# A T5-bias attention kernel gets a new beginning: bias rows copied inside SBUF, last tokens scored first, loads in another order

## The chip, the cores and the metric

One core of a Trainium2 chip runs the whole program. The metric is device time in microseconds (us), the median of several executions. A core has five engines with queues of their own, each worked off strictly in order: PE (matrix products), ACT (exponentials, copies), DVE and POOL (elementwise work), SP (here only the starting of DMAs). [...] DMAs can be started from SP, ACT and POOL.

## The reference

Attention with a relative-position bias, then a mixture of low-rank adapters on its output. The sizes are B = 8 batches, H = 8 heads, S = 576 tokens, D = 64.

```python
scores = q @ k.T / sqrt(D) + bias_table[bucket(|i - j|)]   # per batch and head
attn = softmax(scores)
x = (attn @ v) as (B*S, H*D)                               # (4608, 512)
logits = x @ w_gate                                        # 8 experts, the best 2 chosen
out = x + sum over the 2 of softmax weight * (x @ A[e]) @ B[e]
```

From a distance of 128 tokens on all buckets are the last one, so a bias relative to the last bucket is zero there.

## The kernel before, in words

**Units.** A unit is a batch and a pair of heads; there are 32 (`NU`), four (`HP`) to a batch, taken in order. The 576 tokens are split into 512 main tokens and 64 last ones ("tail"). For each unit q and k are loaded (`load`, fp32 staging with four buffers each), cast to bf16 (`cast`, mostly on POOL), and turned by PE (`turn`, whose PSUM result DVE copies out). The tails of a whole batch are loaded at once (`load_tail`, two buffers), cast by `cast_tail`, and turned as an item of the same `turn`.

**Scores.** `edges(u)` scores the main tokens against the last ones and the other way round, one PSUM tile and one exponential of 128x1024 (`pt`). `keys(u, c)`, for c in 0, 2, 1, 3, scores 128 keys against 512 queries for two heads; the bias near the diagonal is added by four more matmuls from the table `Wt` (a Toeplitz-like row, shifted by one from partition to partition) against `anti`, and ACT exponentiates it into `pk`. `edges`, `keys` and `turn` share three PSUM tiles in rotation (`score_tile`); V products and small items share two others (pool `mp`). The bias of the edges is not added but multiplied after the exponential: `edge_l` (POOL) by the factors `EL`, `edge_t` (DVE) by `ET`, and the corner (last tokens against last tokens) by `EC` in `corners_bias` (POOL).

**The bias tables.** The 8x32 bias table is loaded, turned into rows `gx` (8x520) and `gp` (8x7x128, seven shifted and strided copies) by DVE and POOL. `gp` is written to DRAM (`gd`), and `table(h)` reads unit 0's part of `Wt` back for each head, 64 partitions each a shifted piece; `table_rest` reads the parts of the other three head pairs. `gx` is written to DRAM too (`gnd`), `table_n` reads `Wn`, and `factors_l`, `factors_t` and the second half of `corners_first` multiply it by `anti` and let ACT exponentiate EL, ET and EC.

**V products.** `step(u, j)` (j = 0, 1) multiplies the probabilities by V with a column of ones (`values`), and `normalise` divides. Around these steps the loop puts the matmuls of the adapters.

**Order.** It is written out by hand; there is no scheduler. Every engine's queue has the order of the source lines. The loop over u runs from 0 to 29; in round u the order is: casts for unit u+2 and v of unit u+1 on POOL (`prep`), tail loads and `load(u+4)` on SP, `edges(u)`, two `keys(u)`, `step(u-1, 0)`, `edge_l`, `edge_t`, two more `keys(u)`, `turn` of unit u+2, `step(u-1, 1)`. `prep` also casts the tails of batch 2 at u = 3 (table `tq`), and the adapter weights are cast by POOL in the same round (`weights_cast`). The last two units have their own code. A DMA from SP or ACT is released only when the DMA eight places before it in program order has landed.

The lines that matter below: L112 (q loads), L109 (k and v loads), L129 and L123 (tail loads), L141 and L137 (casts), L149 and L153 (tail casts), L201 (`table`), L205 (`table_rest`), L210 (`table_n`), L371 and L373 (turn: PE, DVE copy), L423 and L428 (keys: products, bias), L431 (exponential of keys), L500 and L502 (edges: PE, exponential), L507 (`edge_l`), L644 (`gp` to DRAM), L275 (weights cast).

Of the kernel before, what the change touches and what calls it, by code (L numbers as in the profile page):

```python
# [38 lines left out]
def kernel(  # L39
# [76 lines left out]
    def load_tail(b, names="qkv", g0=0, g1=HP):  # L116
        eng = nc.sync
# [45 lines left out]
    load_tail(0, "qk", 0, 1)  # L163
# [9 lines left out]
    nc.vector.memset(gp, 0.0)  # L173
    bts = cp.tile([H, NB], FP32, tag="bts")
# [3 lines left out]
    lo, runs = half, []  # L178
    for d in range(half + 1, FAR + 1):
        if d == FAR or buckets[d] != buckets[lo]:  # L180
            runs.append((lo, d))
            lo = d
    for i, (lo, d) in enumerate(runs):
        eng = (nc.vector, nc.gpsimd)[i % 2]
        eng.tensor_copy(gx[:, C + lo:C + d],
                        bts[:, buckets[lo]:buckets[lo] + 1].to_broadcast((H, d - lo)))
    nc.vector.tensor_copy(gx[:, C - FAR + 1:C], _ap(gx, C + FAR - 1, [[-1, FAR - 1]]))
    x0, xn = (C - FAR) // 4 - 1, FAR // 2 + 2
    nc.vector.tensor_copy(gp[:, :, x0:x0 + xn], _ap(gx, 4 * x0 + 1, [[1, 7], [4, xn]]))
    gd = nc.dram_tensor("g_d", (H, 7, GY), BF16, kind="Internal").ap()  # L190
# [9 lines left out]
    def table(h, eng):  # L200
        eng.dma_start(out=Wt[h * 64:h * 64 + 64, 0, :WN],  # L201
                      in_=_dram(gd, h * 7 * GY, [[1, 32], [2 * GY, 2], [1, WN]]))
# [4 lines left out]

# [8 lines left out]
    def factors_l():  # L216
        ps = score_tile("fl")
        for hp in range(HP):
            for e in range(2):
                for h in range(2):  # L220
                    rows = slice(h * 64, h * 64 + 64)
                    for f in range(2):
                        nc.tensor.matmul(ps[f * 64:f * 64 + 64, h, hp * 64 + e * 32:hp * 64 + e * 32 + 32],
# [3 lines left out]
        nc.scalar.activation(EL.rearrange("p g h x -> p h g x"),  # L227
                             ps[:, :, :HP * 64].rearrange("p h (g x) -> p h g x", g=HP), ACT.Exp,
                             scale=scale)

    def factors_t():
        ps = score_tile("ft")
        pst = ps.rearrange("p h (g x) -> p h g x", x=64)
        for hp in range(HP):
            for e in range(2):
                for h in range(2):
                    rows = slice(h * 64, h * 64 + 64)
                    nc.tensor.matmul(pst[64:, h, 2 * hp + e, :], lhsT=turned(h),
                                     rhs=Wn[rows, hp, 129 - e:193 - e],
                                     start=(hp == 0 and e == 0), stop=True,  # L240
                                     skip_group_check=True)
        nc.scalar.activation(ET[64:].rearrange("p g h x -> p h g x"),  # L242
                             ps[64:].rearrange("p h (g x) -> p h g x", g=HP), ACT.Exp, scale=scale)

    def presets():
        nc.vector.memset(ET[:64], 1.0)
        for t in pts:
            nc.gpsimd.memset(t[:, :64], 0.0)
        for i in range(2):
            nc.gpsimd.memset(tvs[i], 0.0)  # L250
            nc.gpsimd.memset(pcs[i], 0.0)
# [15 lines left out]
    def weights_load():  # L267
        nc.sync.dma_start(out=A4f.rearrange("p e c r -> p e (c r)"),
                          in_=moe_A.rearrange("e (p c) r -> p e (c r)", c=4))
        nc.sync.dma_start(out=G4f.rearrange("p c e -> p (c e)"),  # L270
                          in_=moe_w_gate.rearrange("(p c) e -> p (c e)", c=4))
        nc.sync.dma_start(out=Bf, in_=moe_B.rearrange("e r d -> (e r) d"))
# [195 lines left out]
    def corners_first(b):  # L468
        sc = score_tile("cn")
        n = HP * 64  # L470
        corner_scores(b, sc[:, 0, :n], 0, HP, True)
        for hp in range(HP):
            for e in range(2):
                for h in range(2):
                    rows = slice(h * 64, h * 64 + 64)
                    nc.tensor.matmul(_ap(sc[rows, 0, :], n + hp * 64 + e, [[2, 32]]),
                                     lhsT=Wn[rows, hp, 1 - e:65 - e], rhs=turned(h)[:, :32],
                                     start=False, stop=True, skip_group_check=True)
        px = ep.tile([128, HP, 64], BF16, name="pcx", tag="pcx")
        nc.scalar.activation(px.rearrange("p g i -> p (g i)"), sc[:, 0, :n], ACT.Exp, scale=scale)  # L480
        nc.scalar.activation(EC, sc[:, 0, n:2 * n], ACT.Exp, scale=scale)
        return px
# [159 lines left out]

    cast(0, "q", nc.scalar)
    nc.scalar.dma_start(out=gd, in_=gp)  # L644
    load(1, "qk")
    load(0, "v")
    cast_tail(0, "qk", nc.gpsimd, 0, 1)
    cast(0, "k", nc.gpsimd)
    turn([qk_item(0), tl_item(0, 0, 1)])
    for h in range(2):  # L650
        table(h, nc.scalar)
    nc.sync.dma_start(out=gnd, in_=gx)
    load_tail(0, "qk", 1)
    load_tail(0, "v")
    for h in range(2):
        table_n(h, nc.sync)
    cast_tail(0, "qk", nc.gpsimd, 1)
    presets()
    cast(1, "q", nc.vector)
    cast(1, "k", nc.vector)  # L660
# [11 lines left out]
    cast(0, "v", nc.gpsimd)  # L672
    cast_tail(0, "v", nc.gpsimd)

    tturn = {max(4 * c - 4, 2): c for c in range(1, B)}
    tload = {max(w - 2, 0): c for w, c in tturn.items()}
# [6 lines left out]
    def prep(u):  # L683
        b, hp = units[u]
        if u + 2 < NU:
            for nm in ("q", "k") if u > 0 else ("k",):
# [36 lines left out]
    for u in range(NU - 2):  # L723
        b, hp = units[u]
        open_probs(u)
        if u:
            prep(u)
        if u in tload:
            load_tail(tload[u])
        if u == 1:  # L730
            weights_load()
        if u + 4 < NU:
            load(u + 4)
        if u == 3:
            weights_cast()
# [3 lines left out]
        if u in (4, 5):  # L739
            weights_turn(u - 4)  # L740
# [235 lines left out]
```

## Time and profile before

| | |
|---|---|
| median of 3 runs | 200.79 us (199.09 to 200.93) |
| the profiled execution: time, span | 200.43 us, 198.6 us |
| busy: PE, DVE, ACT, POOL | 168.4, 131.1, 163.0, 124.0 us |
| DMA | 40.82 MB, 206 GB/s over the span |
| mean granted TensorE clock | 0.961 |

The span runs from the first to the last instruction on the core. A row of the timeline has the start, the time, the engine (a q behind it means its queue, where DMAs are issued), the line, the operation, output and input, and in brackets how long the engine had been idle and what ended that.

### The profile page before, as it was taken

What the parts mean: (1) busy time and instruction counts of PE and PEld (TensorE: products, weight loads), DVE (VectorE), ACT (ScalarE), POOL (GpSimd) and SP (SyncE); (2) the same over time, 40 slices, a digit from 0 to 9 for tenths busy, and PEclk for the clock granted to TensorE, in tenths of its full rate; (3) what the DMA queues carried; (4) which work ended last, traced back from release to release, by engine and by line L of the source; (5) the groups of instructions that cost most, each with busy time, mean ns of one, the idle gap of its engine ahead of it and who ended that gap; (6) DMA issues with size and microseconds to landing.
All of it is one profiled execution on the core that took longest, in us unless ns stands there. A gap on an engine that the chain in (4) does not pass through costs nothing. (4 is left out here: it accounts for less than half of the span.)

```text
span 198.6 us, 9888 instructions
## 1 busy us (share of the span) xinstructions
PE 168.4 (85%) x4230; PEld 128.1 (65%) x4253; DVE 131.1 (66%) x327; ACT 163.0 (82%) x204; POOL 124.0 (62%) x303
## 2 busy tenths in 40 slices
PE   0364999999999999999999999999999999996660
PEld 0233666777777777776777777776777777875430
DVE  4411244476577778788877787778786887896541
ACT  3148589999999999999999999999999999982331
POOL 4298543876586859594949494959585847243510
PEclk9999589999999999999999999999999999999965
DMA  5878989888888688857888888778898511132425
GB/s 136 219 217 261 233 214 251 259 251 239 242 240 244 163 250 275 264 154 235 222 262 245 244 265 251 219 184 250 254 296 264 161 56 53 56 104 75 149 95 169
DMA packets 68515, 40.82 MB, mean 206 GB/s; under 512 B 22248, under 2 KB 63736, under 8 KB 68472
## 3 DMA queue, kind: packets, MB, share of 16 engines
q1 hardware_dynamic: 67752, 39.77, 69.2%
q8 instruction: 33, 0.54, 1.1%
q10 hardware_dynamic: 720, 0.43, 0.8%
q14 instruction: 10, 0.08, 0.1%
HBM read 30.72 MB, written 9.46 MB: 202 GB/s over the span
## 5 line engine op out<-in xcount | busy, mean ns | idle before, releaser
L431 ACT ACTIVATE pk<-sc 128x1024 bf16<-128x1024 f32 x120 | 113.5, 1035 | 4.2 <-PE sc L428 4.2
L423 PE MATMUL sc<-tx 64*64 64x512 bf16 x480 | 49.5, 400 | 0.0
L373 DVE COPY tx<-tx 128x2048 bf16<-128x2048 bf16 (+8 forms) x36 | 36.3, 1007 | 15.0 <-PE tx L371 13.3
L526 PE MATMUL pv<-v,pk 128*128 128x65 bf16 x992 | 41.7, 194 | 4.1 <-PE sc L428 1.9
L428 PE MATMUL sc<-Wt,anti 64*64 64x256 bf16 x480 | 41.9, 307 | 3.2 <-DMA Wt<-g_d 3.2
L502 ACT ACTIVATE pt<-sc 128x1024 bf16<-128x1024 f32 x32 | 32.8, 1024 | 12.5 <-PE sc L500 6.7
L526 PEld LDWEIGHTS <-pk 128*128 128x128 bf16 x1024 | 37.7, 98 | 7.4 <-issue 1.8
L566 DVE TENSOR_TENSOR xn<-pv,rc 128x320 bf16<-128x320 f32 x62 | 30.5, 491 | 2.1
L565 DVE RECIPROCAL rc<-pv 128x5 f32<-128x5 f32 x62 | 11.9, 192 | 20.3 <-PE pv L573 11.0
L589 POOL TENSOR_TENSOR a<-z,top 128x16 f32<-128x16 f32 (+2 forms) x16 | 3.5, 222 | 34.4 <-DVE top L579 30.8
L304 DVE TENSOR_TENSOR ot<-dl,xn 128x512 f32<-128x512 f32 x26 | 17.9, 689 | 10.4 <-PE sc L428 9.4
L423 PEld LDWEIGHTS <-tx 64*64 64x64 bf16 x480 | 16.3, 108 | 10.2 <-issue 1.1
L428 PEld LDWEIGHTS <-anti 64*64 64x64 bf16 x480 | 18.5, 110 | 4.0 <-issue 3.9
L141 POOL CAST qn<-qs 128x512 bf16<-128x512 f32 x29 | 17.8, 612 | 4.8 <-DMA qs<-in_q_dram 4.8
L371 PEld LDWEIGHTS <-qn 64*128 64x128 bf16 x256 | 7.8, 97 | 20.0 <-issue 7.7
L137 POOL CAST v<-vs 128x512 bf16<-128x512 f32 x32 | 19.9, 623 | 0.9 <-PE pv L545 0.8
L141 POOL CAST kn<-ks 128x512 bf16<-128x512 f32 x31 | 19.0, 613 | 0.3 <-DMA ks<-in_k_dram 0.2
L371 PE MATMUL tx<-ident,qn 64*128 64x64 bf16 x256 | 9.7, 196 | 10.5 <-ACT qn L141 4.9
L543 PE MATMUL pv<-v,pt 128*128 128x65 bf16 x248 | 17.8, 195 | 0.0
L534 PE MATMUL pv<-vb,pt 128*128 128x130 bf16 x124 | 17.6, 225 | 0.0
L512 DVE TENSOR_TENSOR pt<-pt,ET 128x256 bf16<-128x256 bf16 x32 | 13.3, 415 | 4.1 <-ACT ET L242 4.1
L507 POOL TENSOR_TENSOR pt<-pt,EL 128x128 bf16<-128x128 bf16 x32 | 13.8, 432 | 0.7 <-ACT pt L502 0.2
(133 smaller groups left out, 286.5 us busy)
## 6 DMA issues: line engine op xcount, KB each, us to landing
qs<-in_q_dram SPq DMA_DIRECT2D x32, 256.0 KB, 3.7
vs<-in_v_dram SPq DMA_DIRECT2D x64, 128.0 KB, 4.1
out_dram<-ot SPq DMA_DIRECT2D x32, 256.0 KB, 2.6
ks<-in_k_dram SPq DMA_DIRECT2D x62, 128.0 KB, 4.0
vt<-in_v_dram SPq DMA_DIRECT2D x16, 128.0 KB, 3.5
out_dram<-ot SPq DMA_DIRECT2D x8, 128.0 KB, 3.1
qkt<-in_q_dram SPq DMA_DIRECT2D x7, 128.0 KB, 3.9
qkt<-in_k_dram SPq DMA_DIRECT2D x7, 128.0 KB, 4.0
```

Source lines behind the costliest of these rows:

```text
L137: eng.tensor_copy(t[:, :, :, :D].rearrange("p c h d -> p h c d"), s)
L141: copy(t.rearrange("p c h d -> p h c d"), s)
L304: nc.vector.tensor_tensor(ot.rearrange("p (g x) -> p g x", g=HP), dl.rearrange("p (g x) -> p g x", g=HP), x[:, j, :, 2 * f:2 * f + 2, :].r ...
L373: nc.vector.tensor_copy(sb[:, :n], ps.rearrange("p a (c i) -> p c a i", i=64)[:, :n])
L423: nc.tensor.matmul(sc[prt, h, :], lhsT=kT[rows, c * 128 + f * 64:c * 128 + f * 64 + 64], rhs=qT[rows, :], start=True, stop=False, skip_gro ...
L428: nc.tensor.matmul(_ap(sc[prt, h, :], p0, [[128, 4], [1, n]]), lhsT=turned(h), rhs=_ap(Wt[rows, hp, :], (1 - e) * GY + y0, [[GY, 4], [1, n]]),
L431: nc.scalar.activation(probs[u][0][:, c, :, :], sc, ACT.Exp, scale=scale)
L502: nc.scalar.activation(probs[u][1][:, 64:], sc.rearrange("p h x -> p (h x)"), ACT.Exp, scale=scale)
L526: nc.tensor.matmul(pv[:, o:o + W1], lhsT=pk_slice(u, c, h, j + 2 * f), rhs=vm[:, c, h, :], start=first, stop=False, skip_group_check=True)
L534: nc.tensor.matmul(_ap(pv, h * W1, [[130, 2], [1, W1]]), lhsT=probs[u][1][:, x0:x0 + 128], rhs=tvs[b % 2][:, 2 * hp + h].rearrange("p f d ...
L543: nc.tensor.matmul(pv[:, o:o + W1], lhsT=probs[u][1][:, x0:x0 + 128], rhs=vts[u % NV][:, c, h, :], start=False, stop=False, skip_group_che ...
L566: nc.vector.tensor_tensor(xs[b][:, j, hp], _ap(pv, 0, [[W1, 5], [1, D]]), _ap(rc, 6 * j, [[1, 5], [0, D]]), op=ALU.mult)
```

## The change

The loop starts at u = 3; what rounds 0 to 2 did is written out ahead of it in a new order. In it:

- `table(h)` copies straight from `gp` in SBUF, two DMAs per head, one for every second partition, from SP (h = 1) and ACT (h = 0). `gp` still goes to DRAM, from SP, for `table_rest`.
- The row `gx` is exponentiated once (`ge`, 8x520) and written to DRAM; `Wn` then holds exponentials, and DVE copies EL, EC and ET from PSUM instead of ACT exponentiating them.
- `edges(0)` and `edges(1)` come ahead of unit 0's keys; `edges(2)` ahead of unit 1's. The first V products come after unit 1's keys.
- Nine matmuls on zeros run on PE at the very start.
- Loads: the tails of batch 0 whole at once; k of unit 1 from ACT; q of unit 2 ahead of the tables; v tails of batch 0 and the adapter weights from POOL; v loads later; tails of batch 2 (q, k, v) after q and k of unit 6 and v of unit 5.
- DVE makes all runs of `gx`, and clears the `vb` tiles (128x1040 each) ahead of that; POOL clears `pc`.
- In the loop only the places of `weights_cast` (after `edge_l` of u = 3) and `weights_turn` (end of u = 4, and u = 5) differ.

```diff
     def table(h, eng):
-        eng.dma_start(out=Wt[h * 64:h * 64 + 64, 0, :WN],
-                      in_=_dram(gd, h * 7 * GY, [[1, 32], [2 * GY, 2], [1, WN]]))
+        for i in range(2):
+            eng.dma_start(out=Wt[h * 64 + i:h * 64 + 64:2, 0, :WN],
+                          in_=_ap(gp[h:h + 1], 2 * GY * i, [[1, 32], [1, WN]]))
...
+    def cast_half(u, nm, h, eng):
+        if h == 0:
+            nat[(u, nm)] = qkp.tile([128, 4, 2, D], BF16, name=f"{nm}n", tag=f"{nm}n")
+        copy = eng.copy if eng is nc.scalar else eng.tensor_copy
+        copy(nat[(u, nm)][:, :, h, :], stage[(u, nm)][:, h].rearrange("p (c d) -> p c d", c=4))
+
+    busy = mp.tile([128, 512], FP32, name="busy", tag="mm")
+    for _ in range(9):
+        nc.tensor.matmul(busy, lhsT=zero[:, :128], rhs=zero, start=True, stop=True, skip_group_check=True)
...
     cast(0, "q", nc.scalar)
-    nc.scalar.dma_start(out=gd, in_=gp)
-    load(1, "qk")
+    cast_tail(0, "qk", nc.gpsimd, 0, 1)
+    load(2, "q")
+    table(1, nc.sync)
+    table(0, nc.scalar)
+    nc.sync.dma_start(out=gd, in_=gp)
+    nc.scalar.activation(ge, gx, ACT.Exp, scale=scale)
+    nc.scalar.dma_start(out=gnd, in_=ge)
+    load(2, "k")
     load(0, "v")
...
     turn([qk_item(0), tl_item(0, 0, 1)])
...
+    cast(1, "q", nc.vector)
+    open_probs(0)
+    open_probs(1)
+    edges(0)
+    turn([qk_item(1), tl_item(0, 1, HP)])
+    edges(1)
     for h in range(2):
         table_n(h, nc.sync)
...
     for h in range(2):
         for i in range(2):
             table_rest(h, i, nc.sync)
-    load(2, "qk")
+    load(3, "qk")
     load(1, "v")
-    load(3, "qk")
+    load_tail(1, "qk")
+    load(4, "qk")
     load(2, "v")
+    presets()
+    load_tail(0, "v", eng=nc.gpsimd)
+    weights_load(nc.gpsimd)
+    nc.vector.memset(ET[:64], 1.0)
+    cast(2, "q", nc.vector)
+    cast(2, "k", nc.vector)
+    cast(0, "v", nc.gpsimd)
+    load_tail(1, "v")
+    load(5, "qk")
     load(3, "v")
+    for c in KO:
+        keys(0, c)
+    turn([qk_item(2)])
+    open_probs(2)
+    factors_l()
+    edges(2)
+    edge_l(0)
+    keys(1, KO[0])
+    factors_t()
+    edge_t(0)
+    keys(1, KO[1])
+    load(4, "v")
+    load(6, "qk")
+    px = corners_first(0)
+    cast_tail(0, "v", nc.gpsimd)
+    corners_bias(0, px)
...
+    for c in KO[2:]:
+        keys(1, c)
+    cast(3, "q", nc.gpsimd)
+    cast(3, "k", nc.gpsimd)
+    step(0, 0)
+    keys(2, KO[0])
+    cast(1, "v", nc.gpsimd)
+    load(5, "v")
+    load_tail(2)
+    step(0, 1)
+    keys(2, KO[1])
+    turn([qk_item(3)])
...
+    load(6, "v")
+    keys(2, KO[2])
+    step(1, 0)
+    keys(2, KO[3])
+    turn([qk_item(4), tl_item(1)])
+    step(1, 1)
...
-    for u in range(NU - 2):
+    for u in range(3, NU - 2):
```

The order of POOL's work in rounds 3 and 4 is now: q, k of unit 5, v of unit 4, tail casts (qk of batch 2, v of batch 1), `edge_l(3)`, the three weight casts, q, k of unit 6.

More of the change, by code (lines that the diff above doesn't have):

```diff
@@ L468, in corners_first @@
     def corners_first(b):
[L469 to L478, printed above, removed]
+        ps = mp.tile([128, 512], FP32, name="cn", tag="mm")[:, :HP * 64]
+        corner_scores(b, ps, 0, HP, True)
         px = ep.tile([128, HP, 64], BF16, name="pcx", tag="pcx")
-        nc.scalar.activation(px.rearrange("p g i -> p (g i)"), sc[:, 0, :n], ACT.Exp, scale=scale)
-        nc.scalar.activation(EC, sc[:, 0, n:2 * n], ACT.Exp, scale=scale)
+        nc.scalar.activation(px.rearrange("p g i -> p (g i)"), ps, ACT.Exp, scale=scale)
         return px
```

135 lines of the change are left out of this document (62 added, 73 removed).

## The prediction

> **What bounds the kernel now.** I read the 40 slices first, then the windows, then each engine in order of time.
>
> ```profile
> ACT  3148589999999999999999999999999999982331
> DMA  5878989888888688857888888778898511132425
> ```
>
> ACT, which exponentiates, is full from slice 6 to slice 34. Five exponentials make a unit (one `edges`, four `keys`), and 32 units run one after the other. So the question is when ACT first gets fed without holes, and whether it stays fed.
>
> ```profile
> L431 ACT ACTIVATE pk<-sc 128x1024 bf16<-128x1024 f32 x120 | 113.5, 1035 | 4.2 <-PE sc L428 4.2
> ```
>
> That is 113.5/120 = 0.946 us for each exponential in a row; one unit is 4.7 us and a little more.
>
> ```profile
> 5.19 0.60 ACTq L644 DMA_DIRECT2D g_d<-gp  x1
> 7.64 1.44 ACTq L201 DMA_DIRECT2D Wt<-g_d  x2
> ...
> 12.73 1.94 ACT L431 ACTIVATE pk<-sc 128x1024 bf16<-128x1024 f32 x2 [2.57 <-PE sc L428]
> ...
> 17.05 0.41 ACT L481 ACTIVATE EC<-cn 128x256 bf16<-128x256 f32 x1
> 17.31 0.63 ACT L227 ACTIVATE EL<-fl 128x512 bf16<-128x512 f32 x1
> 17.96 1.02 ACT L242 ACTIVATE ET<-ft 64x1024 bf16<-64x1024 f32 x1
> 21.39 1.02 ACT L502 ACTIVATE pt<-sc 128x1024 bf16<-128x1024 f32 x1 [2.41 <-PE sc L500]
> ...
> 32.42 1.02 ACT L502 ACTIVATE pt<-sc 128x1024 bf16<-128x1024 f32 x1 [0.18 <-issue]
> ...
> 42.59 1.02 ACT L502 ACTIVATE pt<-sc 128x1024 bf16<-128x1024 f32 x1 [0.24 <-DVE rc L565]
> ```
>
> The holes of the beginning are here: ACT waits for the bias table (until 12.73), spends 2.06 us on the factors EC, EL, ET, and waits for unit 1's projections (until 21.39). The edges of units 3 and 5 start at 32.42 and 42.59, 5.1 us a unit. The changed kernel enters its loop at unit 3 in the state that the old one has there (units 0 to 2 exponentiated, units 0 and 1 multiplied by V, q and k of unit 4 turned), and runs nearly the same loop. So the change is worth what those starts move.
>
> But DMA is nearly full too, and at 35 us it sets POOL's pace:
>
> ```profile
> 0.00:5.00 5.00, 0.12 (x6) 0.12 (x8) 2.13 (x14) 1.90 (x2) 2.15 (x15) 1.00 0.53 137
> 5.00:10.00 5.00, 1.91 (x34) 1.01 (x33) 2.44 (x5) 0.86 (x1) 1.30 (x4) 1.00 0.80 218
> 10.00:15.00 5.00, 3.21 (x46) 1.78 (x49) 0.89 (x1) 2.14 (x4) 4.76 (x18) 1.00 0.78 221
> 15.00:20.00 5.00, 1.91 (x80) 1.53 (x72) 0.98 (x2) 3.96 (x6) 4.10 (x9) 0.91 0.88 259
> 20.00:25.00 5.00, 4.84 (x79) 3.50 (x83) 1.50 (x5) 2.86 (x3) 2.81 (x5) 0.50 0.92 234
> 25.00:30.00 5.00, 5.00 (x116) 3.19 (x108) 2.40 (x7) 4.38 (x5) 2.21 (x4) 0.91 0.84 213
> 30.00:35.00 5.00, 4.62 (x118) 3.37 (x115) 2.46 (x7) 4.82 (x6) 1.79 (x3) 1.00 0.89 243
> 35.00:40.00 5.00, 4.56 (x114) 3.76 (x117) 2.19 (x7) 4.93 (x7) 4.56 (x9) 1.00 0.90 268
> ```
>
> (The last two columns are the share of the 16 DMA engines and GB/s.)
>
> ```profile
> 35.31 0.61 POOL L149 CAST qkb<-qkt 128x512 bf16<-128x512 f32 x1 [1.73 <-DMA qkt<-in_k_dram]
> 35.87 1.29 POOL L153 CAST vb<-vt 64x512 bf16<-64x512 f32 x2
> ...
> 38.65 0.42 POOL L507 TENSOR_TENSOR pt<-pt,EL 128x128 bf16<-128x128 bf16 x1
> ...
> 39.57 0.61 POOL L141 CAST kn<-ks 128x512 bf16<-128x512 f32 x1
> ```
>
> POOL waits for the last tokens of batch 2 until 35.31, then works through its queue until k of unit 6 is cast at 40.18. PE turns that k at once:
>
> ```profile
> 40.46 0.28 PE L371 MATMUL tx<-ident,kn 64*128 64x64 bf16 x8
> ```
>
> So at unit 4 the old kernel already stands 0.28 us from a DMA limit: landing of that load, plus 4.87 us on POOL, is the turn of unit 6.
>
> **The change part by part.**
>
> *The beginning.* The table for unit 0 no longer goes through DRAM: the wait from 5.19 (g_d issued) to 7.64 (it can be read back) goes. Against that, DVE now clears two 128x1040 tiles ahead of the bias rows and makes all 15 runs itself.
>
> ```profile
> 1.15 0.43 DVE L173 MEMSET gp<- 8x448 uint32 x1
> 3.16 0.23 DVE L175 TENSOR_SCALAR bts<-btT 8x32 f32<-8x32 f32 x1 [1.58 <-DMA btT<-in_bias_table_dram]
> 3.50 0.66 DVE L185 CAST gx<-bts 8x3 bf16<-8x3 f32 x8
> 4.73 0.43 DVE L189 COPY gp<-gx 8x462 bf16<-8x462 bf16 x1
> 7.49 0.91 DVE L246 MEMSET ET<- 64x1024 bf16 x1 [0.15 <-issue]
> ```
>
> After the clears of `zero` (0.28, as `gx` by its width), gx and gp, near 1.86, two clears at 0.93 (from 0.91 for 1024 columns) end near 3.7, 0.5 later than bts could start; 7 more runs at 0.66/8 cost 0.6, of which 0.35 was a wait for POOL anyway. gp is ready near 5.9 instead of 5.16. The four copies leave on ACT and SP from 5.9 to 7.2 and, at the 3.1 to 3.7 us that table loads take, land by 9.0 to 10.9.
>
> ```profile
> Wt<-g_d SPq DMA_DIRECT2D x4, 114.0 KB, 3.1
> ...
> Wt<-g_d ACTq DMA_DIRECT2D x2, 76.0 KB, 3.7
> ```
>
> Unit 0's edges start near 8.9 (the last-token loads are four times larger, but ACT issues its two copies earlier), unit 1's near 11.4, unit 0's keys near 12.3. From 11.4, 14 exponentials and one corner take 14 x 0.946 + 0.4 = 13.6 us, to 25.0. I add 1.6 for the rest of the table (issued to 14.3, so it lands at 17.4, when ACT would have wanted it near 16) and 1.2 for the four V products of units 0 and 1 that PE now has to fit between unit 2's keys. Unit 3's edges: about 27.8 instead of 32.42, bounds 26 and 31.5: the later one if PE keeps the 0.50 clock that the 20 to 25 us row shows, the earlier one without the holes. The factors leave ACT (one 8x520 row instead, at 7.3 where ACT is idle); DVE's six copies of them lie under keys of unit 1. That is 4.6 us gained, up to here. The nine warm-up matmuls run before 5.1, where PE has nothing else.
>
> *The loads.* The built program lets a DMA of SP or ACT go only when the one eight places before it has landed, as before. In the new order the last tokens of batch 2 come after q, k of unit 6 and v of unit 5, not before unit 6; the MoE weights and the last v tokens of batch 0 go through POOL's own queue. Bytes that SP's stream needs ahead of the cast at 35.31: 512 KB more (q, k of unit 6). POOL's order in unit 3 is unchanged up to there: q5, k5, v4, then this cast; after it vb, EL, the three weights, q6, k6 — the same 4.87 us. So units 4 and later can gain only as much as this load lands earlier.
>
> ```profile
> 28.08 0.38 SPq L112 DMA_DIRECT2D qs<-in_q_dram  x1
> ...
> 30.56 0.60 SPq L129 DMA_DIRECT2D qkt<-in_q_dram  x1
> 31.21 0.64 SPq L129 DMA_DIRECT2D qkt<-in_k_dram  x1
> ...
> 33.93 0.57 SPq L112 DMA_DIRECT2D qs<-in_q_dram  x1
> ...
> 36.61 0.47 SPq L112 DMA_DIRECT2D qs<-in_q_dram  x1
> ```
>
> By issue: the five DMAs of a unit take 2.48 (28.08 to 30.56) to 2.68 us (33.93 to 36.61), at most 0.54 each, one of last tokens 0.65 (30.56 to 31.21). SP after: gp at 5.9, two table copies 1.3, g_d 0.6, k2 and v0 2.0, Wn 1.3, rest of the table 2.55, waits for landings 0.65: 14.3. Ahead of the load in question stand 22 DMAs of units at 0.54 and five of last tokens at 0.65, 15.1 us; with 0.6 for waits by the eight-places rule (my choice) it is issued near 30.0 and lands 4.1 later (31.21 to 35.31): 34.1. By bytes: full-rate time used to 35.0 was the sum of share x 5, 28.2 us; 512 KB more at 268/0.90 GB/s is 1.7, so 29.9. With POOL's queue filling 10 to 17 us (shares 0.78 there now), 0.94 from 5 us on gives 34.0, and 0.89, what 30 to 35 had, gives 35.6. I take 34.3. Gain: 35.31 - 34.3 + 0.28 = 1.3 us. What the beginning gains beyond that is given back as a wait of PE for POOL at unit 4; the beginning may be some 2 us later than worked out and cost nothing. (EL of unit 3 stands behind this cast on POOL, 0.56 + 1.29 + 0.42 us, ready at 36.6; unit 4's first V product, which needs it, would be due some 1.5 us after unit 4's edges at 27.8 + 5.1, at 34.4.)
>
> *POOL's DMAs.* No row shows one. SP's take 0.4 to 0.65 us, POOL's longest instruction now is the 1.29 above: five cost 2 to 6.5 us from 9 us on. POOL's next work, v of unit 0, lands near 14, so up to 5 us are hidden; the rest falls in the 2 us of slack. I charge nothing, and 0 to 1 in the range.
>
> *The copies out of two partitions.* All 156 KB come from partitions 0 and 1. Lower bound of their price: as the DRAM loads above. Upper: if one sixteenth of the machine serves them, 268/0.90/16 = 18.6 GB/s, 8.4 us, landed at 15 instead of 10, and the four loads on SP behind them (each waits for one of them) 5 us late. I take the lower, since their issue and size are nearest to those rows, and keep the upper as a rival. [...]
>
> *Sum.* Profiled span 198.6; the profiled execution took 200.43, so 1.83 lies around it.
>
> ```profile
> core 0: 198.6 us, clock 0.961
> ```
>
> 198.6 - 1.3 + 1.83 = 199.1 us. The median of the three runs, 200.79, is 0.36 above that execution. Under 1%, about 2 us, this kernel's measurement tells no difference.
>
> **Rivals.** (a) *The load stream runs earlier.* If SP is through the tables by 13 and DMA keeps a share of 0.98 (for: the 5 to 15 us windows have room, and POOL's queue fills it; against: 0.92 is the best window of the first 40 us), the load lands at 32.8 and the gain is 2.8: 197.6. It can't be the whole 4.6, for that needs a landing at 31.0, a microsecond after its issue.
> (b) *Nothing reaches the end.* With a share of 0.89 the load lands at 35.6, 0.3 later than now, which the 0.28 covers, and unit 4 waits for POOL exactly where it does now: 200.4, though unit 3 starts 4 us sooner.
> (c) *Slower: the copies inside SBUF.* If the four land after 11.6 instead of 10, SP, which waits for each of them before v0 and Wn, runs late by the difference, and at 1.3 us of it the gain is gone. At the upper price, 5 us less 1 that POOL's queue moves meanwhile, the stream is 4 late: 199.1 + 4 = 203.1. For: two partitions are all of the source. Against: each copy is only 39 KB.
>
> **How the numbers follow.** Forecast 0.38 (198.3 to 200.0), (a) 0.30, (b) 0.12, (c) 0.20. Faster by over 1% means below 198.4: all of (a) and a fifth of the forecast, 0.38. Slower by over 1%: (c) but for its mild part, 0.17. The rest, 0.45. The range for 8 in 10 takes in most of (a), down to 196.3, and most of (c), up to 202.6.
>
> **What would show it.** Right: unit 3's edges at 26 to 31.5, PE's turn of unit 6 waiting for POOL, POOL's cast of batch 2's last tokens waiting for DMA until 33.5 to 35, and from unit 5 on a constant lead of 1 to 2 us. The copies: unit 0's first bias matmul at 9.5 to 11 (right) or after 12 (rival c). Wrong: a lead above 3 us at unit 6, or unit 3 not ahead, or units longer than 5.3 us in the middle of the run.

## The result, and the profile after

The changed kernel takes 210.04 us (median of 4 executions, 207.84 to 211.93), the kernel before 200.86 us beside it. The ratio is 1.045, 95% interval 1.030 to 1.060: slower, where 199.1 us and a range up to 202.6 were forecast. The profiled execution, the fastest of the four, took 207.84 us (200.43 before); the times inside the changed kernel are from it.

The slices of the page after:

```profile
ACT  3146197866999999999999999999999999985230
DMA  6999999999986659986888878878897731123425
```

ACT was to be full earlier. It is full from slice 11, where it was from slice 7, with one deep hole in slice 5; and the DMA engines stand at 9 from slice 2 to 11, where they were at 7 to 9. The span is 206.1 us, 7.5 longer.

ACT in order of time (start, us, engine and line, operation, idle time before and what ended it); L497 are the edges, one for each unit:

```profile
10.49 1.02 ACT L497 ACTIVATE pt<-sc 128x1024 bf16<-128x1024 f32 x1 [2.05 <-PE sc L495]
...
25.02 1.02 ACT L497 ACTIVATE pt<-sc 128x1024 bf16<-128x1024 f32 x1 [6.08 <-PE sc L495]
...
35.68 1.02 ACT L497 ACTIVATE pt<-sc 128x1024 bf16<-128x1024 f32 x1 [0.81 <-PE sc L495]
...
50.59 1.02 ACT L497 ACTIVATE pt<-sc 128x1024 bf16<-128x1024 f32 x1 [0.82 <-DVE xn L561]
...
55.68 1.02 ACT L497 ACTIVATE pt<-sc 128x1024 bf16<-128x1024 f32 x1 [0.23 <-DVE rc L560]
```

Unit 3's edges start at 35.68 (before 32.42), unit 5's at 50.59 (42.59), unit 6's at 55.68, 5.09 us later, as in the kernel before. So 3.3 us are lost up to unit 3, another 4.7 in units 3 and 4, and none after (by the end of the span 0.5 us is back). All 8.0 us lie in the first 50.

The place of the first loss, in windows of 1 us (the last three columns are the granted clock, the share of the 16 DMA engines, and GB/s), and the DMA issues from 4 to 20 us with KB and median time to landing:

```profile
9.00:10.00 1.00, 0.31 (x8) 0.23 (x8) 1.00 (x2) 0.00 (x0) 0.96 (x7) 0.50 0.99 32
10.00:11.00 1.00, 1.00 (x30) 0.74 (x26) 0.15 (x1) 0.51 (x1) 0.87 (x7) 0.50 0.86 27
11.00:12.00 1.00, 0.14 (x6) 0.00 (x0) 0.82 (x1) 0.51 (x1) 1.00 (x2) 0.50 0.71 22
12.00:13.00 1.00, 0.87 (x16) 0.43 (x16) 0.85 (x2) 0.07 (x1) 1.00 (x2) 0.50 0.94 39
```

```profile
Wt<-g_d SPq DMA_DIRECT2D x4, 114.0 KB, 7.0
...
vs<-in_v_dram SPq DMA_DIRECT2D x2, 128.0 KB, 7.9
...
Wn<-gn_d SPq DMA_DIRECT2D x2, 96.5 KB, 7.4
Wt<-gp SPq DMA_DIRECT2D x2, 38.0 KB, 4.8
Wt<-gp ACTq DMA_DIRECT2D x2, 38.0 KB, 6.4
```

For four microseconds the engines are 71 to 99% busy and move 22 to 39 GB/s. The four copies are 39 KB each (38.0 in the page's units of 1024 bytes). The loads behind them land 7 to 8 us after their issue, where such loads took 3 to 4 before; those are issued from 11.96 us on, when POOL's five loads (from 10.71) are on the engines too, and e3 below tells which of the two does it. ACT's longest hole, the 6.08 us ahead of unit 2's edges, is PE waiting for one of them, the row of factors:

```profile
22.39 0.24 PE L229 MATMUL fl<-anti,Wn 64*64 64x32 bf16 x2 [4.09 <-DMA Wn<-gn_d]
```

SP, in order of time:

```profile
8.73 3.19 SPq L109 DMA_DIRECT2D ks<-in_k_dram  x2
11.96 2.03 SPq L109 DMA_DIRECT2D vs<-in_v_dram  x2
15.00 1.28 SPq L215 DMA_DIRECT2D Wn<-gn_d  x2
16.32 2.55 SPq L211 DMA_DIRECT2D Wt<-g_d  x4
...
32.09 2.47 SPq L109 DMA_DIRECT2D vs<-in_v_dram  x4
...
38.09 0.61 SPq L128 DMA_DIRECT2D qkt<-in_q_dram  x1
38.74 0.64 SPq L128 DMA_DIRECT2D qkt<-in_k_dram  x1
```

SP is past the tables, that is, has issued the last of their loads, at 18.87. The values of unit 3 are the first of the row at 32.09; the row at 17.05 issued them before. Batch 2's last keys go at 38.74, before at 31.21. The rows of before for the start of that stretch:

```profile
12.81 0.60 SPq L112 DMA_DIRECT2D qs<-in_q_dram  x1
...
17.05 2.70 SPq L109 DMA_DIRECT2D vs<-in_v_dram  x4
```

POOL of the changed kernel, where both are cast, and PE:

```profile
37.69 0.62 POOL L136 CAST v<-vs 128x512 bf16<-128x512 f32 x1 [3.64 <-PE sc L432]
...
42.84 0.61 POOL L148 CAST qkb<-qkt 128x512 bf16<-128x512 f32 x1 [1.70 <-DMA qkt<-in_k_dram]
```

```profile
40.08 0.29 PE L375 MATMUL tx<-ident,qn 64*128 64x64 bf16 x8 [1.85 <-POOL qn L140]
...
47.87 0.29 PE L375 MATMUL tx<-ident,kn 64*128 64x64 bf16 x8 [0.27 <-POOL kn L140]
```

POOL stands twice: 3.64 us for unit 3's values, ahead of unit 3's round (the row names a PE matmul, but in e5, e7 and e9 the same wait names the load), and 1.70 us within the round for the last tokens. Behind the first stand the casts that PE's turn of unit 5 needs, behind the second EL's multiply of unit 3 (at 44.77) and the casts of unit 6.

### The profile page after: what moved, and what is told of

The parts are those of the page before. It is cut to its first block, busy times and chain, and to the rows that moved or that the text cites. A ratio compares the mean times of both kernels' runs of the same rounds, so it can differ in the third digit from the quotient of the medians.

```text
span 206.1 us, 9916 instructions
## 1 busy us (share of the span) xinstructions
PE 173.2 (84%) x4239; PEld 129.1 (63%) x4262; DVE 136.6 (66%) x343; ACT 162.5 (79%) x203; POOL 124.8 (61%) x300
## 5 line engine op out<-in xcount | busy, mean ns | idle before, releaser
L427 PE MATMUL sc<-tx 64*64 64x512 bf16 x480 | 50.1, 404 | 0.0
L497 ACT ACTIVATE pt<-sc 128x1024 bf16<-128x1024 f32 x32 | 32.8, 1025 | 16.4 <-PE sc L495 14.3
L521 PEld LDWEIGHTS <-pk 128*128 128x128 bf16 x1024 | 37.8, 98 | 8.2 <-issue 2.2
L427 PEld LDWEIGHTS <-tx 64*64 64x64 bf16 x480 | 16.6, 109 | 9.5 <-issue 0.7
L432 PEld LDWEIGHTS <-anti 64*64 64x64 bf16 x480 | 18.6, 111 | 2.4 <-DMA Wt<-gp 1.9
L140 POOL CAST kn<-ks 128x512 bf16<-128x512 f32 x30 | 18.4, 612 | 0.0
L538 PEld LDWEIGHTS <-pt 128*128 128x128 bf16 x256 | 14.2, 99 | 0.0
```

The source lines that it names most:

```text
L140: copy(t.rearrange("p c h d -> p h c d"), s)
L427: nc.tensor.matmul(sc[prt, h, :], lhsT=kT[rows, c * 128 + f * 64:c * 128 + f * 64 + 64], rhs=qT[rows, :], start=True, stop=False, skip_gro ...
L432: nc.tensor.matmul(_ap(sc[prt, h, :], p0, [[128, 4], [1, n]]), lhsT=turned(h), rhs=_ap(Wt[rows, hp, :], (1 - e) * GY + y0, [[GY, 4], [1, n]]),
L497: nc.scalar.activation(probs[u][1][:, 64:], sc.rearrange("p h x -> p (h x)"), ACT.Exp, scale=scale)
L521: nc.tensor.matmul(pv[:, o:o + W1], lhsT=pk_slice(u, c, h, j + 2 * f), rhs=vm[:, c, h, :], start=first, stop=False, skip_group_check=True)
L538: nc.tensor.matmul(pv[:, o:o + W1], lhsT=probs[u][1][:, x0:x0 + 128], rhs=vts[u % NV][:, c, h, :], start=False, stop=False, skip_group_che ...
```

## The experiments

The first four runs tell two theories apart. Theory 1 was that the copies out of two partitions cost most of it; theory 2 that the loads through POOL's queue and the new order do. From e7 on, theory A is that the order on each queue decides (SP's, then POOL's), and theory B that the bytes through POOL's queue do. All ratios are to the kernel before, run beside them.

**e1: the table through DRAM again.**

```diff
-    table(1, nc.sync); table(0, nc.scalar)      # four copies gp -> Wt
     nc.sync.dma_start(out=gd, in_=gp)
     nc.scalar.activation(ge, gx, ACT.Exp, scale=scale)
+    for h in range(2): table(h, nc.scalar)      # gd -> Wt, 64 partitions each
     nc.scalar.dma_start(out=gnd, in_=ge)
```

> The changed kernel, but unit 0's rows of the table go through DRAM again: gp is written to gd by one DMA on SP's queue, the table is read from gd by two DMAs of 64 partitions on ACT's queue, behind the exponentials of the one row of factors. Theory 1 (the four copies out of two SBUF partitions hold the 16 DMA engines from 6 to 13 us, and every later load with them): the 1 us windows between 8 and 13 us move over 100 GB/s instead of 22 to 39, the rest of the table is issued by 14 to 15 us instead of 18.9, unit 3's edges begin before 31 instead of 35.68, and the time is 199 to 202. Theory 2 (the loads put on POOL's queue and the new order of the loads cost most of it, the copies a little): the rest of the table is still issued after 17, unit 3's edges begin after 33, the time is 205 to 208.

Measured: 208.36 us, ratio 1.035 (1.027 to 1.043). Theory 2's number, yet the clogging is gone: the windows from 8 to 13 us move 92 to 336 GB/s. SP, POOL and PE of this kernel:

```profile
12.47 1.27 SPq L214 DMA_DIRECT2D Wn<-gn_d  x2
13.78 3.90 SPq L210 DMA_DIRECT2D Wt<-g_d  x4
```

```profile
41.13 0.62 POOL L148 CAST qkb<-qkt 128x512 bf16<-128x512 f32 x1 [3.28 <-DMA qkt<-in_k_dram]
```

```profile
43.55 0.40 PE L528 MATMUL pv<-vb,pt 128*128 128x130 bf16 x2 [3.10 <-POOL pt L501]
```

SP has issued the first values by 8.52 and then stands until 12.47 for `gn_d`: the row of factors, now exponentiated on ACT, is written there behind the two reads of the table, which themselves wait for `gd`. This wait is of the edit's own making. In the changed kernel the row is written behind copies that need nothing from DRAM, and SP waits 0.9 us for it; with faster copies (e5, below) it doesn't wait there. So e1 takes away the copies and puts another wait in their place, and doesn't price them; e7 does. And the last row shows how lateness becomes time: PE waits 3.10 us for EL's multiply, and POOL has that behind a cast that waits for the last tokens of batch 2.

**e2: the kernel before, with the copies alone.**

```diff
-        eng.dma_start(out=Wt[h*64:h*64+64, 0, :WN], in_=_dram(gd, ...))
+        for i in range(2):
+            eng.dma_start(out=Wt[h*64+i:h*64+64:2, 0, :WN], in_=_ap(gp[h:h+1], 2*GY*i, ...))
```

> The kernel before with one edit: unit 0's rows of the table are copied out of gp inside SBUF by four DMAs on ACT's queue, where two DMAs read them from gd (gd is still written, ahead of them, for the rest of the table). Theory 1 (the copies alone cost most of the 7 to 9 us): 204 to 208, with the windows after the copies' issue under 60 GB/s. Theory 2 (POOL's loads and the order of loads): 200 to 202, since unit 0's bias then only comes late for unit 0, and unit 1 waits for later loads anyway.

Measured: 203.56 us, 1.015 (1.009 to 1.021), between the two expectations. In the kernel before, the copies alone cost some 3 us. Its DMA issues from 5 to 20 us:

```profile
Wt<-gp ACTq DMA_DIRECT2D x4, 38.0 KB, 5.0
```

**e3 and e4: POOL's five loads back on SP**, with the copies (e3) and without (e4).

```diff
-    load_tail(0, "v", eng=nc.gpsimd); weights_load(nc.gpsimd)
+    load_tail(0, "v"); weights_load(nc.sync)
```

> The changed kernel with the copies inside SBUF kept, but the first batch's last values and the weights (five DMAs, 0.8 MB) are issued by SP at the same place of the program instead of by POOL. Theory 1 (copies): 206 to 210, no better than 2 us under the changed kernel, since the stall from 6 to 13 us stays and SP has 3 us more to issue. Theory 2 (POOL's queue takes the DMA engines from 13 to 17 us ahead of the factors' rows and the rest of the table): the table of the factors (Wn) lands within 4 us of its issue instead of 7.4, and the time is 200 to 204.

> The changed kernel with both edits: table through DRAM, first batch's last values and weights on SP. Theory 1: as the first of these four within 1 us, 199 to 202, for the copies were the cost. Theory 2: clearly below it, 198 to 201 against 205 to 208. If it stays over 204, neither of the two is the main cost, and the order of the loads or the longer way of the first bias through DVE is.

Measured: 211.12 us, 1.050 (1.044 to 1.056), and 209.00 us, 1.041 (1.034 to 1.047). Neither gains over its partner (the changed kernel, and e1). E4 fell in its third case, over 204, but that doesn't clear the two suspects, for the reason is a new wait. In e3 (e4's row is alike):

```profile
31.25 0.60 POOL L152 CAST vb<-vt 64x512 bf16<-64x512 f32 x1 [10.09 <-DMA vt<-in_v_dram]
```

The first batch's last values, put at the same place of the program but 18 DMAs behind the first values on SP's queue, come at 31 and hold up POOL. So the times of these runs say nothing on what the bytes on POOL's queue cost; e13 does. But the trace of e3 answers what its expectation asked, for there the copies stay and POOL's loads are gone. DMA issues from 4 to 20 us:

```profile
Wt<-g_d SPq DMA_DIRECT2D x4, 114.0 KB, 3.0
...
vs<-in_v_dram SPq DMA_DIRECT2D x2, 128.0 KB, 3.4
Wn<-gn_d SPq DMA_DIRECT2D x2, 96.5 KB, 3.3
```

These took 7.0, 7.9 and 7.4 us in the changed kernel. So late landings are the work of POOL's bytes, and `Wn` is the load that ACT's hole of 6.08 us ends on: unit 2's edges start at 20.29 here, not 25.02. What the copies do is hold up SP's issue, which is the same in both: the row of k at 8.60 takes 3.28 us here (3.19 there), and SP is past the tables at 19.06 (18.87).

**e5: is it the copying, or the one partition?** Each row of the copies is read from its own partition of a cleared tile `zs`. This kernel leaves out unit 0's bias near the diagonal.

```diff
-                          in_=_ap(gp[h:h + 1], 2 * GY * i, [[1, 32], [1, WN]]))
+                          in_=zs[h * 64 + i:h * 64 + 64:2, :])
```

> The changed kernel with the same four copies inside SBUF (same sizes, same destinations, same queues), but each of the 128 rows is read from its own partition of a cleared tile instead of 64 rows from one partition; unit 0's bias near the diagonal is left out by that. If reading 64 rows out of one partition is what makes the copies slow, they land 2 to 3 us after issue and the windows from 8 to 13 us move over 100 GB/s instead of 22 to 39. If any copy inside SBUF is slow, whatever it reads, they take 4.8 and 6.4 us as before and the windows stay under 50 GB/s.

Measured: 205.65 us (one execution, 201.23 for the kernel before beside it). DMA issues from 4 to 20 us:

```profile
Wt<-zs SPq DMA_DIRECT2D x2, 38.0 KB, 2.6
Wt<-zs ACTq DMA_DIRECT2D x2, 38.0 KB, 2.6
```

2.6 us instead of 4.8 and 6.4, and 185 GB/s from 8 to 13 us where the changed kernel moved 68. Reading out of one partition is what is slow. SP of this kernel:

```profile
10.67 1.30 SPq L218 DMA_DIRECT2D Wn<-gn_d  x2
12.02 2.55 SPq L214 DMA_DIRECT2D Wt<-g_d  x4
```

With the copies spread, SP is past the tables at 14.57, 4.3 us earlier than in the changed kernel. So both theories hold in part: the copies cost SP its time at the tables, POOL's loads the landings behind them.

**e7: no copies, and the row of factors written ahead of the table's reads.**

```diff
     nc.scalar.activation(ge, gx, ACT.Exp, scale=scale)
+    nc.scalar.dma_start(out=gnd, in_=ge)
     for h in range(2): table(h, nc.scalar)
-    nc.scalar.dma_start(out=gnd, in_=ge)
```

> The changed kernel with the table through DRAM, and the one row of factors written to gn_d ahead of the two reads of the table on ACT's queue instead of behind them; POOL's loads stay. Theory A (SP's queue: what counts is when SP is past the factors' rows and the tables, 12.8 us before, 17.7 with the table through DRAM, 19.5 in the changed kernel; the loads behind it, values of unit 3 and last tokens of batch 2, come that much later, POOL's casts wait for them in order, and unit 3's multiply by EL stands behind them): the factors' rows are issued at 8.5 to 9.5 instead of 12.5, SP is past the tables by 14.5, batch 2's last keys are issued by 32.5 (36.0 and 38.7), unit 5's edges begin at 44 to 46 (49.2 and 50.6), time 201 to 204. Theory B (the loads on POOL's queue and the DMA engines' share): SP is past the tables early, but the loads land late all the same, unit 5's edges begin after 48, time 206 to 209.

Measured: 206.23 us, 1.024 (1.017 to 1.031), against 1.045 with the copies. SP is past the tables at 13.46, as theory A wanted, but unit 5's edges are at 49.19, and the time is theory B's. POOL and PE of this kernel, and its DMA queues from 13 to 18 us (packets, MB, share of the engines):

```profile
33.12 0.62 POOL L136 CAST v<-vs 128x512 bf16<-128x512 f32 x1 [4.05 <-DMA vs<-in_v_dram]
```

```profile
35.51 0.39 PE L374 MATMUL tx<-ident,qn 64*128 64x64 bf16 x8 [2.91 <-POOL qn L140]
```

```profile
q1 hardware_dynamic: 533, 0.55, 56.1%
q0 software_dynamic: 192, 0.48, 46.4%
```

q0 is POOL's queue. The kernel before in the same 5 us:

```profile
q1 hardware_dynamic: 1799, 1.22, 80.6%
```

What SP won at the tables went to POOL's loads: SP's queue moves 0.55 MB where it moved 1.22. Its loads land 8 us after issue, and SP, whose DMAs go only when the eighth before has landed, issues three from 17.79 to 24.30: unit 3's queries, issued at 13.51, land after 8.4 us, and the eighth DMA behind them goes at 21.93. (In the trace of the changed kernel the DMAs of SP and ACT share eight landing semaphores; of the 147 issues for which the landing of the DMA before on the same semaphore is recorded none came ahead of it, the closest 0.02 us behind.) POOL stands for unit 3's values, PE for the casts behind them.

**e13: e7 without POOL's loads; e8: e7 with the last tokens earlier; e11: e8 with unit 3's values earlier too; e9 and e12: the same two moves in the changed kernel.**

```diff
 # e13
+    load_tail(0, "v")                 # SP, right behind load(0, "v")
-    load_tail(0, "v", eng=nc.gpsimd); weights_load(nc.gpsimd)
     load_tail(2)
+    weights_load(nc.sync)
 # e8, e9
+    load_tail(2, "qk")
     load(4, "v"); load(6, "qk"); load(5, "v")
-    load_tail(2)
+    load_tail(2, "v")
 # e11, e12, besides
+    load(3, "v")
     load_tail(1, "v"); load(5, "qk")
-    load(3, "v")
```

> e7_rows_first with POOL's loads taken away: the first batch's last values are loaded by SP behind the first values, the weights by SP behind batch 2's last tokens; the order of all else stays. Theory A (each queue's order alone): 205 to 207, as e7, since unit 3's values and batch 2's last tokens stand where they stood. Theory B (POOL's bytes): in e7 SP is past the tables at 13.5, but waits from 17.8 to 24.3 while loads land 7 to 8 us after their issue; without POOL's 0.8 MB they land in 3 to 4, unit 3's values are cast by 30 (33.1), batch 2's last keys issued by 31 (34.6), unit 5's edges begin at 44 to 46 (49.2), time 202 to 204.5.

> The same as e7_rows_first, and the last queries and keys of batch 2 are loaded ahead of the values of unit 4 and the loads of unit 6, seven DMAs earlier. Theory A: batch 2's last keys are issued by 29, POOL's cast of them no longer waits, unit 5's edges begin at 42 to 44, time 198.5 to 201.5. Theory B: as e7 within 1 us.

> e8_rows_tails with one more edit: the values of unit 3 are loaded ahead of the last values of batch 1 and the queries and keys of unit 5, five DMAs earlier. Theory A (order on POOL): in e8 POOL waits 4.07 us for these values until 32.87, the casts of unit 5's queries and keys stand behind, and PE waits 2.69 us for them ahead of unit 4's edges (38.73, 37.35 before). Now that wait is gone or under 1 us, unit 4's edges begin at 36 to 37.5, unit 5's at 42.5 to 44, time 200.5 to 203. Theory B (the loads as a whole are late because POOL's 0.8 MB go ahead of them, and their order matters little): then POOL waits for the queries of unit 5 instead, unit 4's edges stay after 38, time 203.5 to 205.

> The changed kernel with that one edit alone: batch 2's last queries and keys seven DMAs earlier on SP's queue, the copies inside SBUF kept. Theory A: their issue moves from 38.1 to about 33, POOL's cast of them from 42.84 to about 41.2 (the 1.70 us that POOL waits there), and only that much comes off, since the values of unit 3, cast at 37.69 after a wait of 3.64 us, stand ahead of it on POOL: 205.5 to 207.5. Theory B: no gain, 207 to 209.

> The changed kernel with the order of loads alone mended (batch 2's last queries and keys seven DMAs earlier, unit 3's values five earlier); copies inside SBUF, POOL's loads and the row of factors stay. Theory A: 204.5 to 206.5, for the waits of 3.64 and 1.70 us on POOL in the changed kernel go down, but the stream is 4 to 5 us late at its start. Theory B: no gain over e9, 207.5 to 210.

Measured: e13 203.32 us, 1.014 (1.009 to 1.019); e8 204.20, 1.017 (1.013 to 1.020); e11 203.00, 1.012 (1.004 to 1.020); e9 209.26, 1.044 (1.038 to 1.050); e12 207.37, 1.032 (1.026 to 1.038). So POOL's bytes cost e7 about 1% (e13 came out as theory B said), and so do the two places in the order, 0.7% in e8 and 0.5% more in e11. Each of these steps is small enough for the intervals to overlap; the traces are clearer, with unit 5's edges at 49.19 in e7, 46.29 in e13 and 45.42 in e8, and unit 4's at 38.73 in e8 and 36.28 in e11. The times of e8 and e12 lie between what the two theories said, that of e11 at the upper edge of theory A's. In the changed kernel the last tokens alone bring nothing (e9, a miss for both theories: POOL then waits 4.49 us for unit 3's values instead), both places together 1.3% against e16 below and the changed kernel. E11 and e12 differ by the copies alone (and the row of factors that goes with them): 2.0%, as between e7 and the changed kernel, 2.1%.

**e10: everything mended.** e11 with e13's edit.

> All that the runs point to, on the changed kernel: table through DRAM with the row of factors written ahead of its reads, batch 2's last queries and keys seven DMAs earlier, unit 3's values five earlier, the first batch's last values on SP and the weights on SP behind batch 2's last tokens. If the copies, the waiting row, POOL's bytes and the order of loads are the whole cost, POOL's casts wait no longer than in the kernel before, unit 5's edges begin at 40.5 to 43, time 198 to 201. If something else in the change costs (warm-up matmuls and the slower granted clock behind them, the longer way of the bias through DVE, exponentials moved to DVE copies), it stays over 202.

Measured: 205.58 us, 1.022 (1.014 to 1.030), far from the 198 to 201 hoped for and no better than e11 and e13. The weights, now last, are needed by POOL ahead of unit 6's casts. POOL, PE, and windows of this kernel (PE first of the busy times, granted clock third from the end):

```profile
40.00 0.61 POOL L278 CAST A<-A4f 128x512 bf16<-128x512 f32 x1 [2.46 <-DMA A4f<-in_moe_A_dram]
```

```profile
42.06 0.39 PE L374 MATMUL tx<-ident,qn 64*128 64x64 bf16 x8 [2.76 <-POOL qn L140]
```

```profile
42.00:44.00 2.00, 1.77 (x44) 1.53 (x45) 0.52 (x1) 0.00 (x0) 1.52 (x4) 0.50 1.11 302
44.00:46.00 2.00, 2.00 (x27) 1.75 (x24) 1.14 (x3) 0.28 (x1) 0.42 (x1) 0.50 0.97 274
46.00:48.00 2.00, 2.00 (x30) 1.09 (x28) 0.68 (x2) 1.01 (x2) 2.00 (x5) 0.50 0.86 252
```

A wait of PE can cost more than its length: behind it the granted clock is 0.50 for 6 us (1.00 in the windows from 38 to 41), though PE is busy for 5.77 of them. From the turn of k of unit 6 to unit 5's edges it takes 4.37 us (42.62 to 46.99); before, at a granted clock of 1.00, 2.13 (40.46 to 42.59). Of the difference 1.0 us is a turn of the weights that stood elsewhere before (45.11 to 46.13 here).

**e15 and e14: the weights where they were before; e14 with their casts and turns behind unit 6's.**

```diff
 # e15 and e14
+    weights_load(nc.sync)
     load_tail(2, "qk")
 # e14 besides: weights_cast() in unit 4 behind prep(4), not in unit 3
-        if u == 5: weights_turn(1)
+        if u == 5: weights_turn(0); weights_turn(1)
-        if u == 4: weights_turn(0)
```

> e10_all with the weights loaded by SP ahead of batch 2's last queries and keys, behind unit 5's keys, where the kernel before has them. If the late weights were the cost in e10_all, POOL's wait of 2.46 us for them goes, PE does not wait 2.76 us for unit 6's queries, unit 5's edges begin at 43 to 44.5 instead of 46.99, time 200.5 to 202.5. If not, 204 to 206.

> e15_weights_before_tails, and besides POOL casts the weights behind unit 6's queries and keys instead of ahead of them, and both turns of the weights on PE stand in unit 5, behind its first keys, instead of one ahead of unit 5's edges. If waits on POOL and the halved clock behind them are all that is left, PE does not wait over 1 us from 36 to 50, its granted clock stays at 1.00 there, unit 5's edges begin at 41 to 42.5 (42.59 before), the steady part after it is the same as before, time 198.5 to 200.5. If something else in the change costs, 201.5 to 204.

Measured: 203.99 us, 1.015 (1.012 to 1.019), and 203.42, 1.015 (1.010 to 1.019); both missed their better cases. POOL and PE of e14:

```profile
35.85 0.62 POOL L136 CAST v<-vs 128x512 bf16<-128x512 f32 x1 [3.97 <-DMA vs<-in_v_dram]
```

```profile
38.84 0.40 PE L528 MATMUL pv<-vb,pt 128*128 128x130 bf16 x2 [3.79 <-POOL pt L501]
```

Unit 4's edges, at 33.84, are 3.5 us ahead of the kernel before (37.35). Then the next load in the row, the values of unit 4, takes it all: POOL waits for it, EL's multiply stands behind, PE waits 3.79 us.

**e18: those values first, the weights behind unit 6; e17: besides, EL's multiply ahead of the casts that wait.**

```diff
 # e18 and e17
-    weights_load(nc.sync); load_tail(2, "qk"); load(4, "v"); load(6, "qk")
+    load(4, "v"); load_tail(2, "qk"); load(6, "qk"); weights_load(nc.sync)
 # e17 besides, in unit 3
         edge_l(u)
+        cast(4, "v", nc.gpsimd); cast_tail(2, "qk", nc.gpsimd)   # were in prep(3)
```

> e14_weights_late_cast with the values of unit 4 loaded first and the weights last of four: unit 4's values, batch 2's last queries and keys, unit 6's queries and keys, the weights. If only the place of a load counts: unit 4's values are cast by 32.5 instead of 35.85, unit 3's multiply by EL begins at 35 to 36, unit 5's edges at 41.5 to 43, time 199.5 to 201.5. If the bytes count, the wait goes over to batch 2's last tokens, unit 5's edges begin after 43.5, time 201.5 to 204.

> e18_v4_first, and in unit 3 POOL multiplies by EL ahead of the casts of unit 4's values and of batch 2's last tokens, not behind them. If POOL's order behind late loads is all that is left: EL's multiply of unit 3 ends by 34.5 (38.4 in e14), PE waits under 1 us for it, unit 5's edges begin at 40 to 41.5 (44.54 in e14, 42.59 before), time 198 to 200, below the kernel before. If the stream of loads is the bound, POOL waits then for unit 4's values or unit 6's queries, unit 5's edges begin after 42.5, time 200 to 203.

Measured: 200.28 us, 0.998 (0.994 to 1.002), and 200.63 us, 0.997 (0.994 to 1.001): no difference from the kernel before that can be told. (No trace of e17 shows where its waits lie.) ACT and POOL of e18:

```profile
34.39 1.02 ACT L496 ACTIVATE pt<-sc 128x1024 bf16<-128x1024 f32 x1
...
40.09 1.02 ACT L496 ACTIVATE pt<-sc 128x1024 bf16<-128x1024 f32 x1 [0.24 <-DVE rc L559]
...
47.49 1.02 ACT L496 ACTIVATE pt<-sc 128x1024 bf16<-128x1024 f32 x1 [0.24 <-DVE rc L559]
```

```profile
40.21 0.62 POOL L136 CAST v<-vs 128x512 bf16<-128x512 f32 x1 [2.52 <-DMA vs<-in_v_dram]
```

Units 4 and 5 start 3.0 and 2.5 us ahead of the kernel before (37.35, 42.59), unit 6 0.2 ahead (47.67): unit 5's values were late this time. The new beginning, without the copies, does feed ACT sooner, up to unit 5; the stream of loads does not come sooner, and each gain is handed back at the first load that wasn't put ahead.

**e16: no warm-up matmuls.**

```diff
-    for _ in range(9):
-        nc.tensor.matmul(busy, lhsT=zero[:, :128], rhs=zero, ...)
```

> The changed kernel without the nine matmuls on cleared data at the start. In the changed kernel the granted clock is 0.50 from 8 us on all the same; if they bear on nothing, unit 5's edges begin within 0.7 us of 50.59 and the time is within 1.5 us of the changed kernel's. If the clock that they raise is used by the first turns and edges, unit 0's edges come 0.3 to 1 us later than 10.49; if they take power from what follows, the time falls by over 2 us.

Measured: 209.70 us, 1.045 (1.041 to 1.049), the ratio of the changed kernel. Unit 0's edges start at 10.06, not later, and unit 5's at 51.58, 1.0 us later where under 0.7 was foretold; the time is the same, so no gain or cost of these matmuls can be told.

## Why the prediction was wrong

**What held.** `gp` was ready at 6.29 (5.9 foretold). Unit times are those of before from unit 5 on, so the starts of the units decide, and from unit 5 on the difference is constant. POOL's five DMAs took 3.60 us of POOL (10.71 to 14.31; 2 to 6.5 foretold), hidden under a wait. The chain it named, from the cast of batch 2's last tokens to the turn of unit 6, took 42.84 to 47.87, 5.03 us, against 4.87 + 0.28 by its rows. The warm-up matmuls, which the sum gave no worth, show none (e16).

**The step that failed first: the price of the copies.** Two bounds were stated, 3.1 to 3.7 us and 8.4, and the lower was taken, "since their issue and size are nearest to those rows". Measured: 4.8 and 6.4 us each, and 8.3 us from the issue of the first (6.31) to the matmul that waits for the last:

```profile
14.59 0.53 PE L432 MATMUL sc<-Wt,anti 64*64 64x256 bf16 x4 [1.28 <-DMA Wt<-gp]
```

Unit 0's first bias matmul waits for a copy until 14.59; the upper bound had said 15, and the prediction's own sign for rival (c) was a start after 12. The likeness that counted was not size or issue but where they read from: spread over 128 partitions the same copies took 2.6 (e5). 156 KB in 8.3 us are 19 GB/s, where the upper bound had 18.6. The copies' own landing cost ACT little, 1.21 us of idle time ahead of unit 0's keys; more came with it: while they ran, the 16 engines were 71 to 99% busy at 22 to 39 GB/s, and SP's queue stood. The prediction's rival (c) had this: SP "runs late by the difference", 5 us less 1. SP was past the tables at 18.87 instead of 14.3, 4.6 us; with the copies spread it was at 14.57 (e5), so the rest of that sum was right. In time the copies cost about 2% in the changed kernel (e7, e11 against e12).

**The second: the stream behind the tables.** 27 DMAs were to take 15.1 us and 0.6 of waits by the eight-places rule, 15.7. They took from 18.87 to 38.74, 19.9: 4.2 us more. With the copies spread they took 20.8 (e5, 14.57 to 35.38), so this term is not the copies'. The term that failed is the 0.6 us of waits, "my choice": by the prediction's own issue times, 15.1, the waits were 4.8. Two things were left out. POOL's bytes: they were let fill a share of the engines that stood free, and instead took half of them while SP's queue was waiting its turn (e7: 0.48 MB beside 0.55); the same 27 DMAs take 21.1 with them (e7) and 18.15 without (e13, 14.35 to 32.50). And the rate was read from one stretch: the five of a unit at 28 to 30 us; over the long stretch before, from 12.81 to 31.21, 30 DMAs had gone in 18.4 us, 0.61 each and not 0.54. By that rate 27 take 16.6; why e13 still needs 1.6 more no run tells.

The two terms make 8.8 us; the landing took the 4.1 that were taken (38.74 to 42.84). K of unit 6 was turned at 47.87, where the sum had 40.46 - 1.3 = 39.2, 8.7 us later. Rival (c), 203.1, was the right mechanism with the first term alone; with the second it would have said 207.3, and the profiled execution took 207.84. That it comes so near is in part luck: the turn of unit 6 was 8.7 us late, the edges 8.0, the span 7.5.

**Two steps were never priced.** One is the landing of `Wn`, which unit 2's edges stand behind on PE: the sum has its issue, 1.3 us, and nothing for the 7.4 us that it takes beside POOL's bytes (3.3 without them, e3). The other is the place of unit 3's values, behind q and k of units 4 and 5 and no longer ahead of them (32.09 against the row at 17.05): "POOL's order in unit 3 is unchanged up to there" was so for POOL, not for what it waits for.

**What became of the gain.** Unit 3's edges were to start at 27.8 and did at 28.6 and 29.4 once the copies and POOL's loads were gone and unit 3's values came earlier (e14, e18). Of the 4.6 us that the prediction counted up to there, 3.8 and 3.0 exist, then, though with the table through DRAM and not with the copies that were to bring them. It also said that they would be given back where POOL waits for a late load; they were, one load after another. Which share of the slowdown each cost has in the changed kernel can't be told by adding, because one wait covers the next: the copies are 1.5% in the kernel before (e2) and about 2% in the changed one, but mending the last tokens' place is worth nothing there (e9) and 0.7% without the copies (e8 against e7).

## What to carry to other kernels

When work at the start is brought forward, ask whether the loads behind it come forward too; where the DMA engines were already near 0.9, as here, the gain ended at the first load that an in-order engine cast late, and mending that wait uncovered the next. Price a new DMA not only by when it lands but by the share of all engines it holds while it runs, and look at which partitions it reads. Take the rate of a queue from the longest stretch of the trace, not from its tightest one. And when an experiment takes one wait away, see in its trace whether the edit put another in its place, as e1, e3 and e4 did.

## What the hardware showed beyond that

A copy inside SBUF from one partition to 32 lasted 4.8 to 6.4 us for 39 KB in the changed kernel, against 2.6 from 32 partitions (e5). While four of them ran, the engines showed as 71 to 99% busy at 22 to 39 GB/s, and k of unit 2, issued beside them, took 6.6 us to land and SP 3.19 us to issue (1.15 beside the spread copies of e5).

Loads through POOL's queue took nearly half of the DMA engines (46.4%, 13 to 18 us) beside SP's queue (56.1%), whose own loads then landed after 8.1 to 8.6 us instead of 3.9 to 4.2 (e7, before): the weights moved ahead with their queue (issued from 12.25, before from 26.43), at the cost of the others.

The clock: a PE wait of 2.76 us is followed by 6 us at a granted 0.50 (e10), although PE is busy for 5.77 of them. In windows of 0.2 us from 4 to 60 us the clock of the changed kernel changes at 8.0, 18.3, 21.7, 28.5, 42.2 and 45.6 us; the windows of 2 us from 34 to 50 us put the changes of e10 at 34.4, 37.8, 41.2 and 48.0. Within each of these two runs they lie one to four times 3.4 us apart. In e10 the drop at 41.2 came 1.9 us after PE fell idle (39.3), and the return at 48.0, 6.8 us after the drop, 5.9 us after PE was busy again (42.06). Whether the cost of a stall depends on where it falls between such changes was not shown.
